# Small attention values of a fused attention and mixture-of-experts kernel held in free columns of a PSUM bank

## The chip, the cores and the metric

The kernel runs on one core of one Trainium2 chip. The metric is the device time of one execution in microseconds (us); less is better. The core has a matrix engine (TensorE, PE in the profile, PEld for its weight loads), a vector engine (VectorE, DVE), an activation engine (ScalarE, ACT), a general engine (GpSimd, POOL) and a queue engine (SyncE, SP) that issues most of the DMAs. TensorE writes to PSUM, a small memory of eight banks of 512 fp32 columns on 128 partitions; everything else lives in SBUF.

## The reference

Three stages follow each other. Only the first is touched by the change.

```python
# 1 attention: B=4, H=8, 512 local and 32 global positions, head size 64, window 32
s_g = scale * q_g @ concat(k_g, k_l).T            # global queries see all keys
out_g = softmax(s_g) @ concat(v_g, v_l)
s_l = concat(scale * q_l @ k_g.T, where(|i-j| <= 32, scale * q_l @ k_l.T, -1e9))
out_l = softmax(s_l) @ concat(v_g, v_l)           # softmax divides by sum + 1e-9
# 2 experts: 2176 tokens of 512, 8 experts, one expert a token
logits = x @ w_gate; e = argmax(logits)
y = probs[e] * (relu(x @ w1[e]) @ w2[e])
# 3 dense layer 512 -> 2048 -> 512
h = y @ w_in; g = h if h >= 1 else 0 if h <= -1 else (h + 1)**2 / 4
return g @ w_out
```

## The kernel before

Everything is written out by hand: the order of the instructions on TensorE, VectorE, ScalarE and SyncE is the order of the Python code, and a recording layer adds the waits between engines. Each engine works through its own list in order, so a waiting instruction holds up all that stand behind it on that engine.

The attention runs over 32 heads (`h`, one batch entry and head each) and 8 groups of four heads' global queries (`g`). The list `units` puts them into one sequence, and a loop over it issues for each unit pieces of several units, so that the engines work on different heads at one time. The pieces that matter here:

- `s_pair` (L253, L256): TensorE makes the scores of two heads in a PSUM tile `sp`, the mask added last.
- `s_max` (L262, L263): VectorE takes four row maxima of a head's 512 columns into `mx`, and turns them into the biases `mn` of the exponentials.
- `s_exp` (L280): ScalarE makes the exponentials `p` of a head in four instructions, and the sums `ss`.
- `t_head` (L335, L336): TensorE turns `p`, and VectorE copies the result out of PSUM to `pto`.
- `pv` (L380 to L385): TensorE multiplies with the values into `xo`; VectorE adds 1e-9 to the sums, takes the reciprocals `ri`, and multiplies `xo` by them.
- `s_glob`, `g_max`, `g_exp`, `g_norm`, `t_glob`, `pv_glob` (L292, L303 to L305, L316, L322 to L324, L346, L347, L356 to L359): the same for the global queries of a group; `pv_glob` is 24 small products on TensorE into `gxb`, then one multiplication on VectorE.
- `spread_v` (L225 to L227): GpSimd makes shifted copies of the values `v`, three in a row for a pair of heads.
- `route` (L457 to L466): nine steps on VectorE that make the chosen expert and its weight from a batch entry's logits, one of them with an exponential `ex` on ScalarE (L461). They wait in a list `fill`, of which up to eight are issued at the end of a unit.
- `ranks` (L491 to L494): TensorE counts tokens by expert into `gxb`.

`gxb` is one PSUM bank that stays allotted through the attention. Before, four things lie in it: columns 0 to 63 the last global scores (`s_glob`), 128 to 191 the output of `pv_glob`, from 256 on the counts of `ranks`, and 448 to 455 the logits of the global tokens. The recording layer orders accesses to such a tile by the bank, not by columns: an instruction that touches `gxb` waits for the last one on another engine that touched it and stands ahead of it in the code, where one of the two writes.

Of the sequence in one unit, two places matter: `s_max` of a head stands ahead of `pv_glob`, and `t_head` with `s_pair` ahead of both:

```python
        if kind == "h" and a < 31 and a != 3:
            s_max(a)
...
        for q in pend_g:
...
            pv_glob(q)
        for c in pend_v:
            pv(c)
```

After the attention (some 130 us), the expert stage and the dense layer follow, in which TensorE is busy nearly all the time.

Of the kernel before, what the change touches and what calls it, by code (L numbers as in the profile page):

```python
# [8 lines left out]
F32 = mybir.dt.float32  # L9
# [15 lines left out]
B, H, SL, SG, D = 4, 8, 512, 32, 64  # L25
# [8 lines left out]
E, F = 8, 1024  # L34
# [89 lines left out]
def emit(tc, d, out):  # L124
    nc = tc.nc
# [9 lines left out]
    def C(name):  # L135
        lo, hi = COFF[name]
        return csp[:, lo:hi] if hi <= CP else cst[:, lo - CP:hi - CP]
# [35 lines left out]
    ap = at.enter_context(tc.tile_pool(name="ap", bufs=1))  # L173
    ps = at.enter_context(tc.tile_pool(name="ps", bufs=1, space=PSUM))

    ks, vt, pt, ss = {}, {}, {}, {}
# [16 lines left out]
    def dma(o, i):  # L193
        t = nc.sync.dma_start(o, i)
        n = 1
        for z in o.shape:
            n *= z
        moved.append((t, n / 2**17))
        room = ROOM
        for u, n in reversed(moved):  # L200
            room -= n
            if room < 0 and u is not t:
                tc.add_manual_dep(t.ins, u.ins.name, mybir.DependencyInfo(mybir.DependencyClass.Sync, mybir.DependencyReason.DATA), reason="paced")
                break
        return t
# [23 lines left out]
    def v_at(j):  # L229
        g, t = divmod(j, 3)  # L230
        return (NW, 0, 2 * NW)[t] + g
# [10 lines left out]
    gxb = ps.tile([128, 512], F32, name="gxb")  # L242
# [14 lines left out]

    def s_max(n):
        sp = sps[n]
        mx = ap.tile([128, 4], F32, tag="mx4", name="mx4", bufs=2)  # L260
        mn = ap.tile([128, 4], F32, tag="mn", name="mn", bufs=3)
        nc.vector.tensor_reduce(mx, sp, axis=AX.X, op=ALU.max)  # L262
        nc.vector.tensor_single_scalar(mn, mx, -scale, op=ALU.mult)  # L263
        smn[n] = mn
# [101 lines left out]
    L4 = ap.tile([128, 5, 8], F32, name="L4")  # L366
    Lg = L4[:, 4, :]

    def pv(c):
        b, g = divmod(c, 4)  # L370
        p, v = pt.pop(c), vt[c]
        if g == 0:
            xr[b] = ap.tile([128, 4, DM], F32, tag="xr", name="xr", bufs=2)
            xT[b] = ap.tile([128, 4, SL], F32, tag="xT", name="xT", bufs=2)
        xo = ps.tile([128, 4, 2, D], F32, tag="s" if c == 15 else "x", name="xo", bufs=3 if c == 15 else 1)
        for i in range(4):
            for z in range(2):
                for a in range(4):
                    j = 4 * i + a
                    nc.tensor.matmul(xo[a * WIN:(a + 1) * WIN, i, z, :], lhsT=p[:, z, j * WIN:(j + 1) * WIN],  # L380
                                     rhs=v[:, v_at(j), 64 * z:64 * z + 64], start=True, stop=True)
        r = ap.tile([128, 4, 2], F32, tag="ri", name="ri", bufs=3)
        nc.vector.tensor_scalar_add(r, ss[b][:, :, 2 * g:2 * g + 2], 1e-9)
        nc.vector.reciprocal(r, r)
        nc.vector.tensor_tensor(xr[b][:, :, g * 128:(g + 1) * 128].rearrange("p i (z d) -> p i z d", z=2), xo,  # L385
                                r.unsqueeze(3).to_broadcast([128, 4, 2, D]), ALU.mult)

# [59 lines left out]
    def route(b):  # L447
        nt = 4 if b < B - 1 else 5
        t0 = 4 * b
        L = ap.tile([128, 5, 8], F32, tag="L", name="L", bufs=2)[:, 0:nt] if b < B - 1 else L4  # L450
        mx = ap.tile([128, 5, 1], F32, tag="mx", name="mx", bufs=2)[:, 0:nt]
        sc = ap.tile([128, 5, 8], F32, tag="sc", name="sc", bufs=2)[:, 0:nt]
        m2 = ap.tile([128, 5, 1], F32, tag="m2", name="m2", bufs=2)[:, 0:nt]
        ex = ap.tile([128, 5, 8], F32, tag="ex", name="ex", bufs=2)[:, 0:nt]
        se = ap.tile([128, 5, 1], F32, tag="se", name="se", bufs=2)[:, 0:nt]
        V = nc.vector
        ops = [lambda: V.tensor_reduce(L[:, 0:4], lgt[b][:, :, :, 0:E].rearrange("p i c e -> p i e c"), axis=AX.X, op=ALU.add)]  # L457
        rank_b = C("rank").unsqueeze(1).to_broadcast([128, nt, 8])
        ops += [lambda: V.tensor_reduce(mx, L, axis=AX.X, op=ALU.max),
                lambda: V.tensor_tensor(L, L, mx.to_broadcast([128, nt, 8]), ALU.subtract),  # L460
                lambda: (nc.scalar.activation(ex, L, AF.Exp), V.scalar_tensor_tensor(sc, L, 0.0, rank_b, ALU.is_ge, ALU.mult)),  # L461
                lambda: V.tensor_reduce(m2, sc, axis=AX.X, op=ALU.max),
                lambda: V.tensor_tensor(oh[:, t0:t0 + nt, :], sc, m2.to_broadcast([128, nt, 8]), ALU.is_equal),
                lambda: V.tensor_reduce(se, ex, axis=AX.X, op=ALU.add),
                lambda: V.tensor_scalar_add(se, se, 1e-9),
                lambda: (V.reciprocal(gid[:, t0:t0 + nt, 0:1], se),  # L466
                         dma(xs[b * SL:b * SL + nt * 128, DM:XW].rearrange("(i p) f -> p i f", p=128),
                                           gid[:, t0:t0 + nt]))]
        return ops
# [169 lines left out]
    for s in range(len(units)):  # L639
# [23 lines left out]
        if (kind, a) == ("g", 0):  # L663
            s_max(3)
        if kind == "h" and a < 31 and a != 3:
            s_max(a)
        if kind == "h" and a == 30:
            s_max(31)
        elif kind == "g":
            g_max(a)  # L670
# [6 lines left out]
        for c in pend_v:  # L677
            pv(c)
            if nv < 16:
                load_v(nv)  # L680
                nv += 1
            if 0 < c < 14:
                spread_v(c + 2)
            b, g = divmod(c, 4)
            if g % 2:
                tasks.append(lambda b=b, g=g: x_store(b, g // 2))
            tasks.append(lambda b=b, g=g: x_turn(b, g))
            if b < B - 1 and g == 3:
                then = [lambda b=b: tasks.append(lambda: early(b))]
                tasks += [lambda b=b: logits(b), lambda b=b: logits_t(b),  # L690
                          lambda b=b, then=then: fill.extend(route(b) + then)]
# [15 lines left out]
    weigh(xz, 128, nc.gpsimd)  # L707
    t_head(30)
    pv(14)
    t_head(31)  # L710
    for t in tasks:
        t()
    dma(xs[B * SL:N, 0:DM], xrg)
    glob_turn()
    pv(15)
    x_turn(B - 1, 2)
    x_store(B - 1, 1)
# [6 lines left out]
    part3()  # L724
    logits3_t()
    last = route(B - 1)
    for op in last[:6]:
        op()
# [23 lines left out]
    sc = rp.tile([128, NB], F32, name="sc")  # L752
# [716 lines left out]
```

## Time and profile before

| | |
|---|---|
| median of 3 runs | 740.49 us (738.86 to 744.5) |
| the profiled execution's own time | 741.64 us |
| its span, first to last instruction | 739.8 us |
| PE busy | 711.3 us (96%) |
| DVE busy | 486.1 us (66%) |
| ACT busy | 332.1 us (45%) |
| POOL busy | 150.2 us (20%) |
| mean granted TensorE clock | 0.992 of full |

Busy times are of the profiled execution. A busy TensorE is not one at its peak, since matmuls overlap. The chain that ended last names for each moment what was waited for; work of other engines beside it costs nothing. "issue" in that chain is time in which an engine waited for nothing that the profile shows. The time of an execution is its span and some 2 us around it.

### The profile page before, as it was taken

To read this page: it belongs to the slowest core of one execution; us is meant where nothing else is said; L and a number is where in the kernel's file an instruction comes from. 1 tells how busy PE (TensorE), PEld (TensorE's weight loads), DVE (VectorE), ACT (ScalarE), POOL (GpSimd) and SP (SyncE) were. 2 spreads that over 40 slices of the span, in tenths; PEclk is the share of its full clock that TensorE was granted. 3 is DMA by queue.
4 is the path that set the end of the run, shared out by engine and by line. 5 is a ranking of instruction groups with operands and counts; after the bars stand their busy time and mean duration, and the time that the engine had idled before them with its cause. 6 is when DMAs were issued, how large, how long until landed. Compare 5 with 4: busy or idle time off the path is not lost.

```text
span 739.8 us, 16419 instructions
## 1 busy us (share of the span) xinstructions
PE 711.3 (96%) x6609; PEld 637.6 (86%) x6609; DVE 486.1 (66%) x887; ACT 332.1 (45%) x762; POOL 150.2 (20%) x185
## 2 busy tenths in 40 slices
PE   6889888999999999999999999999999999999995
PEld 4666666999999999899998898999989898998984
DVE  4778885674516478875777678758775876645443
ACT  4757664453525457664564543233323332322220
POOL 3445543677641340000000000000000000011112
PEclk9999999999999999999999999999999999999998
DMA  8786666485658578763531321101110100001111
GB/s 280 237 258 202 203 194 186 134 291 196 190 166 301 199 252 305 244 208 104 122 99 58 105 68 57 58 1 58 57 58 1 58 0 1 1 30 57 43 43 71
DMA packets 52254, 96.07 MB, mean 130 GB/s; under 512 B 9817, under 2 KB 27769, under 8 KB 50128
## 3 DMA queue, kind: packets, MB, share of 16 engines
q1 hardware_dynamic: 48704, 84.75, 36.1%
q0 software_dynamic: 3472, 10.25, 4.2%
q8 instruction: 53, 0.87, 0.5%
q14 instruction: 25, 0.20, 0.1%
HBM read 80.28 MB, written 14.75 MB: 128 GB/s over the span
## 4 chain that ended last, share of the span: by engine, by line
PE 79%; issue 8%; DVE 7%; ACT 2%; DMA 2%; POOL 1%; SPq 0%; POOLq 0%; ACTq 0%; DVEq 0%
PE fh L988 7%; PE fh L986 7%; PE fh L987 7%; PE o L988 6%; PE o L987 6%; PE o L986 6%; PE hp L988 4%; PE hp L986 4%; PE hp L987 4%; PE yp L986 4%; PE yp L987 4%; PE yp L988 4%; PE ps_o L335 2%; PE sp L253 2%; DMA ks<-in_k 2%
## 5 line engine op out<-in xcount | busy, mean ns | idle before, releaser
L1318 DVE SCALAR_TENSOR_TENSOR r<-r 128x384 f32<-128x384 f32 (+1 forms) x96 | 51.4, 535 | 113.4 <-ACT r L1317 113.4
L986 PE MATMUL o<-wh,gh 128*128 128x512 f32 x272 | 106.9, 393 | 0.8 <-ACT acc L1367 0.8
L988 PE MATMUL o<-wh,gl 128*128 128x512 f32 x272 | 107.6, 396 | 0.0
L987 PE MATMUL o<-wl,gh 128*128 128x512 f32 x272 | 107.3, 394 | 0.0
L1371 POOL DMA_INDIRECT out_dram<-acc,rid x17 | 16.5, 969 | 446.4 <-DVE acc L1369 444.8
L1320 ACT ACTIVATE gh<-g 128x384 fp32r<-128x384 f32 (+1 forms) x96 | 48.8, 508 | 129.2 <-DVE g L1319 129.2
L988 PE MATMUL fh<-yh,wl 128*128 128x384 f32 (+1 forms) x320 | 104.3, 326 | 0.0
L986 PE MATMUL fh<-yh,wh 128*128 128x384 f32 (+1 forms) x320 | 104.2, 326 | 0.0
L987 PE MATMUL fh<-yl,wh 128*128 128x384 f32 (+1 forms) x320 | 104.2, 326 | 0.0
L1317 ACT ACTIVATE r<-fh,half 128x384 f32<-128x384 f32 (+1 forms) x96 | 54.0, 562 | 105.6 <-PE fh L988 105.0
L986 PEld LDWEIGHTS fh<-yh,wh 128*128 128x128 f32 x320 | 60.2, 188 | 3.5
L987 PEld LDWEIGHTS fh<-yl,wh 128*128 128x128 f32 x320 | 60.2, 188 | 3.4
L988 PEld LDWEIGHTS o<-wh,gl 128*128 128x128 f32 x272 | 51.1, 188 | 12.4 <-DVE gl L1326 0.4
L988 PEld LDWEIGHTS fh<-yh,wl 128*128 128x128 f32 x320 | 60.2, 188 | 0.0
L986 PEld LDWEIGHTS o<-wh,gh 128*128 128x128 f32 x272 | 51.1, 188 | 9.1 <-ACT acc L1367 1.2
L987 PEld LDWEIGHTS o<-wl,gh 128*128 128x128 f32 x272 | 51.1, 188 | 8.1
L280 ACT ACTIVATE p<-sp,mn 128x128 f32<-128x128 f32 x128 | 45.2, 373 | 20.0 <-DVE mn L263 10.1
L1319 DVE TENSOR_TENSOR g<-r,fh 128x384 f32<-128x384 f32 (+1 forms) x96 | 51.0, 532 | 3.3
L986 PE MATMUL yp<-hTh,w2h 128*128 128x256 f32 (+5 forms) x176 | 51.7, 294 | 0.0
L988 PE MATMUL yp<-hTh,w2l 128*128 128x256 f32 (+5 forms) x176 | 51.2, 291 | 0.0
L987 PE MATMUL yp<-hTl,w2h 128*128 128x256 f32 (+5 forms) x176 | 51.1, 290 | 0.0
L1326 DVE TENSOR_TENSOR gl<-g,gh 128x384 fp32r<-128x384 f32 (+1 forms) x96 | 50.7, 529 | 0.0
(238 smaller groups left out, 1617.3 us busy)
## 6 DMA issues: line engine op xcount, KB each, us to landing
w1r<-in_w SPq DMA_DIRECT2D x32, 512.0 KB
w2r<-in_w SPq DMA_DIRECT2D x32, 512.0 KB
wraw<-in_wf SPq DMA_DIRECT2D x16, 1024.0 KB
ks<-in_k SPq DMA_DIRECT2D x16, 400.0 KB
v<-in_v SPq DMA_DIRECT2D x16, 384.0 KB
yr<-ys SPq DMA_DIRECT2D x68, 64.0 KB
qp<-in_q SPq DMA_DIRECT2D x16, 256.0 KB
xs<-xr SPq DMA_DIRECT2D x8, 512.0 KB
```

The costliest lines, as they stand in the source:

```text
L253: nc.tensor.matmul(sps[2 * c + z][a * WIN:(a + 1) * WIN, i, :], lhsT=q[r, j * WIN:(j + 1) * WIN], rhs=k_at(k, r, j), start=(i == 0), stop= ...
L280: nc.scalar.activation(p[:, i, :].rearrange("p (a b w) -> p a b w", a=2, b=2), v, AF.Exp, bias=mn[:, i:i + 1], scale=scale, accum_out=ss[b ...
L335: nc.tensor.transpose(o[:, i, :], p[:, i, :], ident)
L986: nc.tensor.matmul(o, lhsT=ah, rhs=bh, start=first, stop=False)
L987: nc.tensor.matmul(o, lhsT=ah, rhs=bl, start=False, stop=False)
L988: nc.tensor.matmul(o, lhsT=al, rhs=bh, start=False, stop=last)
L1317: nc.scalar.activation(r[:, 0:w], o[:, 0:w], AF.Relu, bias=half, scale=0.5)
L1318: nc.vector.scalar_tensor_tensor(r[:, 0:w], r[:, 0:w], 1.0, r[:, 0:w], ALU.min, ALU.mult)
L1319: nc.vector.tensor_tensor(g[:, 0:w], r[:, 0:w], o[:, 0:w], ALU.max)
L1320: nc.scalar.activation(gh[:, 0:w], g[:, 0:w], AF.Copy)
L1326: nc.vector.tensor_tensor(gl[:, 0:w], g[:, 0:w], gh[:, 0:w].bitcast(F32), ALU.subtract)
L1371: w = nc.gpsimd.indirect_dma_start(out=out, out_offset=bass.IndirectOffsetOnAxis(ap=rid[:, tt:tt + 1].bitcast(U32), axis=0), in_=a, in_off ...
```

## The change

Four SBUF tiles of VectorE's small operations become columns of `gxb`: the row maxima of `s_max` (64 to 71, two sets in turn), the sums with 1e-9 added in `pv` (72 to 79; the reciprocals `ri` stay in SBUF), and in `route` the scores `sc` (80 to 119) and, of the first three batch entries, the logits `L` (192 to 223, one set where there were two). No instruction is added, taken away or reordered on TensorE, VectorE, ScalarE or SyncE. On GpSimd, whose order is not written by hand, the four small copies behind the third `pv_glob` (L362) now stand behind the second copy of a `spread_v` (L226), and before stood ahead of it. From L383 on, lines have a number that is higher by one than before.

```diff
     def s_max(n):
         sp = sps[n]
-        mx = ap.tile([128, 4], F32, tag="mx4", name="mx4", bufs=2)
+        mx = gxb[:, 64 + 4 * (n % 2):68 + 4 * (n % 2)]
         mn = ap.tile([128, 4], F32, tag="mn", name="mn", bufs=3)
...
         r = ap.tile([128, 4, 2], F32, tag="ri", name="ri", bufs=3)
-        nc.vector.tensor_scalar_add(r, ss[b][:, :, 2 * g:2 * g + 2], 1e-9)
-        nc.vector.reciprocal(r, r)
+        e = gxb[:, 72:80].rearrange("p (i z) -> p i z", i=4)
+        nc.vector.tensor_scalar_add(e, ss[b][:, :, 2 * g:2 * g + 2], 1e-9)
+        nc.vector.reciprocal(r, e)
...
-        L = ap.tile([128, 5, 8], F32, tag="L", name="L", bufs=2)[:, 0:nt] if b < B - 1 else L4
+        L = gxb[:, 192:224].rearrange("p (t e) -> p t e", e=E) if b < B - 1 else L4
         mx = ap.tile([128, 5, 1], F32, tag="mx", name="mx", bufs=2)[:, 0:nt]
-        sc = ap.tile([128, 5, 8], F32, tag="sc", name="sc", bufs=2)[:, 0:nt]
+        sc = gxb[:, 80:80 + nt * E].rearrange("p (t e) -> p t e", e=E)
```

What it moves is waits, since VectorE now writes a bank that TensorE writes too. Two places show it. The first is TensorE's list at the fourth `pv_glob`, behind the counts of `ranks` (58.4 us in the profile before); DVE, PE and so on with a number are the semaphores by which an engine tells how far it is, DMAHW those of the loads. Before:

```order
L494 LDWEIGHTS ones
L494 MATMUL gxb<-oh,ones 128x8
L356 MATMUL gxb<-v,pgt 32x64 [waits DMAHW2_49]
L356 MATMUL gxb<-v,pgt 32x64
L356 MATMUL gxb<-v,pgt 32x64 [waits DMAHW0_49]
L356 MATMUL gxb<-v,pgt 32x64 x13
```

And in the change:

```order
L495 LDWEIGHTS ones
L495 MATMUL gxb<-oh,ones 128x8
L356 MATMUL gxb<-v,pgt 32x64 [waits DMAHW2_49,DVE_49]
L356 MATMUL gxb<-v,pgt 32x64
L356 MATMUL gxb<-v,pgt 32x64 [waits DMAHW0_49]
L356 MATMUL gxb<-v,pgt 32x64 x13
```

The first product of `pv_glob` waits for VectorE now: for the `s_max` that stands ahead of it in the code, that is until L263 has read the maxima out of `gxb`. Of the eight `pv_glob`, numbers 1 to 5 and 7 (from 0) have this wait; numbers 0 and 6 wait on VectorE as before.

The second place is VectorE's list in the `route` of the first batch entry (51.4 us in the profile before). Before:

```order
L457 TENSOR_REDUCE L<-lg 128x32
L459 TENSOR_REDUCE mx<-L 128x4 [waits DVE_49]
L460 TENSOR_TENSOR L<-L,mx 128x32 [waits DVE_49]
L461 SCALAR_TENSOR_TENSOR sc<-L,cst 128x32 [waits DMAHW3_49,DVE_49]
L462 TENSOR_REDUCE m_1047<-sc 128x4 [waits DVE_49]
L463 TENSOR_TENSOR oh<-sc,m_1047 128x32 [waits DVE_49]
L464 TENSOR_REDUCE se<-ex 128x4 [waits Activation_49]
L465 TENSOR_SCALAR se<-se 128x4 [waits DVE_49]
```

And in the change:

```order
L458 TENSOR_REDUCE gxb<-lg 128x32
L460 TENSOR_REDUCE mx<-gxb 128x4 [waits DVE_49]
L461 TENSOR_TENSOR gxb<-gxb,mx 128x32 [waits DVE_49]
L462 SCALAR_TENSOR_TENSOR gxb<-gxb,cst 128x32 [waits DMAHW3_49,Activation_49]
L463 TENSOR_REDUCE m_1033<-gxb 128x4 [waits DVE_49]
L464 TENSOR_TENSOR oh<-gxb,m_1033 128x32 [waits DVE_49]
L465 TENSOR_REDUCE se<-ex 128x4
L466 TENSOR_SCALAR se<-se 128x4 [waits DVE_49]
```

The wait for ScalarE's exponential has moved three steps forward, from the sum `se` to the scores, since the exponential reads the bank that the scores are written to.

## Rows read from the trace of the kernel before

**Rows 1.** After the attention: us; PE, PEld, DVE, ACT, POOL busy; granted clock; DMA
```profile
130.00:739.80 609.80, 600.58 (x3587) 556.05 (x3585) 392.47 (x619) 254.37 (x414) 92.17 (x79) 1.00 0.34 110
```

**Rows 2.** Chain that ended last, in order of time: start, us, what (attention)
```profile
41.63 0.93 PE gxb L356 x46
...
47.29 1.93 issue
...
58.41 1.31 PE gxb L356 x48
...
73.76 0.59 PE ps_o L335 x4
...
87.28 0.81 PE gxb L356 x48
...
89.15 0.94 PE sp L292 x16
...
113.61 0.81 PE gxb L356 x48
114.63 1.41 issue
```

**Rows 3.** VectorE's instructions in order of time: start, us, line, output and input
```profile
34.92 0.63 DVE L263 TENSOR_SCALAR mn<-mx 128x4 f32<-128x4 f32 x1
...
42.30 0.24 DVE L263 TENSOR_SCALAR mn<-mx 128x4 f32<-128x4 f32 x1
...
51.95 0.81 DVE L460 TENSOR_TENSOR L<-L,mx 128x32 f32<-128x32 f32 x1
...
54.42 0.17 DVE L465 TENSOR_SCALAR se<-se 128x4 f32<-128x4 f32 x1
...
59.66 0.17 DVE L263 TENSOR_SCALAR mn<-mx 128x4 f32<-128x4 f32 x1
...
73.23 0.17 DVE L263 TENSOR_SCALAR mn<-mx 128x4 f32<-128x4 f32 x1
...
88.53 0.17 DVE L263 TENSOR_SCALAR mn<-mx 128x4 f32<-128x4 f32 x1
...
108.34 0.82 DVE L263 TENSOR_SCALAR mn<-mx 128x4 f32<-128x4 f32 x1
...
115.08 0.17 DVE L263 TENSOR_SCALAR mn<-mx 128x4 f32<-128x4 f32 x1
...
117.99 0.15 DVE L525 TENSOR_SCALAR zt<-n 128x1 f32<-128x1 f32 x1
...
118.65 0.15 DVE L537 TENSOR_SCALAR zidx<-ip 128x1 int32<-128x1 f32 x1
```

**Rows 4.** GpSimd's instructions in order of time, 50 to 56 us
```profile
51.89 0.82 POOL L225 COPY v<-v 96x768 f32<-96x768 f32 x1 [3.35 <-DMA v<-in_v]
...
53.53 0.72 POOL L227 COPY v<-v 64x640 f32<-64x640 f32 x1
```

**Rows 5.** One line's instructions each: least, median and most ns; first and last start
```profile
L263 DVE TENSOR_SCALAR mn<-mx x32: 169/170/821, 7.0 to 115.1; 128x4 f32<-128x4 f32 x32
...
L336 DVE COPY pto<-ps_o x32: 653/681/693, 10.7 to 121.7; 128x512 f32<-128x512 f32 x32
...
L461 ACT ACTIVATE ex<-L x4: 229/230/236, 52.8 to 128.8; 128x32 f32<-128x32 f32 x3, 128x40 f32<-128x40 f32 x1
```

**Rows 6.** All engines in order of time, 34 to 38 us
```profile
34.25 0.88 PE L356 MATMUL gxb<-v,pgt 128*32 128x64 f32 x48
...
35.67 0.37 ACT L280 ACTIVATE p<-sp,mn 128x128 f32<-128x128 f32 x1 [1.49 <-DVE mn L263]
...
36.18 1.37 PE L335 MATMUL ps_o<-ident,p 128*128 128x128 f32 x4
```

**Rows 7.** Busy time in two stretches of 4 us, columns as in rows 1
```profile
54.00:58.00 4.00, 1.91 (x57) 1.33 (x41) 3.72 (x12) 2.37 (x11) 1.07 (x3) 1.00 0.42 131
58.00:62.00 4.00, 4.00 (x75) 2.75 (x77) 3.45 (x11) 3.40 (x17) 2.68 (x7) 0.57 0.88 252
```

## The prediction

> **What bounds the kernel now.** I read the busy times by stage first, then the chain of waits through the attention, then the lists of VectorE and GpSimd side by side. After the attention TensorE is busy 600.58 of 609.80 us [rows 1]. That stage has no slack, and the change touches nothing in it, so it moves as a whole by what the attention's end moves. The 130 us before it are the only place where the change can act. There the chain jumps between TensorE and VectorE [rows 2]: products, then a row maximum, then exponentials, then products again. VectorE is on the path where it does a `route`, TensorE in nearly all the rest. So the question is not how much VectorE saves, but where it saves it, and which engine has to wait in exchange.
>
> **What the change can take away.** L263 works on four columns and has a median of 170 ns, yet one of its 32 took 821 ns [rows 5]. The step L460 took 0.81 us, and began right behind a copy of values on GpSimd (51.89 to 52.71, a batch of three that ends at 54.25) [rows 3, 4]; the other long ones lie under such copies too. These steps read and write SBUF alone. L336, which reads 512 columns of PSUM and writes SBUF, stays within 653 to 693 ns over 32 executions, although GpSimd is copying through many of them [rows 5]. From this I take it that a small step with an operand in PSUM is no longer held by GpSimd. What that is worth, place by place:
>
> - L263 at 108.34 took 0.82 us [rows 3] and its exponentials are waited for: 0.82 − 0.17 = 0.65 us gained on the path.
> - L263 at 34.92 took 0.63 us [rows 3]: 0.46 us gained, which the next part spends.
> - In `route` of the first two entries L460 and two steps behind it are stretched. Once they are short, L461 meets its new wait for `ex`, and L465, which stays in SBUF, meets GpSimd's third copy, which ends at 54.25; it began at 54.42 [rows 3, 4]. Only some 0.15 us is left of each, 0.3 us for both. In the third entry nothing was stretched, and the wait for `ex` (0.23 us [rows 5], plus 0.1 us until VectorE sees it) costs 0.33 us.
> - The other stretched L263 and L383 are beside the path. I cost them at nothing, covered by the loads of keys up to 16 us and by TensorE's own work later; uncovered, they would be a gain of at most 0.3 us each.
>
> Together: −0.65 − 0.3 + 0.33 = −0.6 us.
>
> **What it adds: waits.** Six of the eight `pv_glob` now wait until L263 of the `s_max` ahead of them has read the bank. Behind the waiting product stands everything of TensorE: `pv`, `t_head`, the next scores. From the end of an L263 to the engine that it releases takes some 0.1 us (34.92 + 0.63 = 35.55, ScalarE starts at 35.67 [rows 3, 6]). With L263 at its short 0.17 us, a `pv_glob` can start 0.27 us after L263's start:
>
> - Number 1: 34.92 + 0.27 = 35.19, it started at 34.25 [rows 3, 6]: 0.94 us late. But the `t_head` behind it had slack: it stood at 36.18 for 1.37 us because it was fed one exponential at a time [rows 6], where an unhindered one takes 0.59 us [rows 2], and the exponentials now come 0.46 us earlier. I take +0.1 us.
> - Number 2: 42.30 + 0.27 = 42.57 against 41.63: +0.9 us [rows 2, 3]. [...] I take 0, and keep 0.9 for the range.
> - Number 3: 59.66 + 0.27 = 59.93 against 58.41: 1.5 us [rows 2, 3]. [...] I take +0.75 us, and 1.5 as the end.
> - Number 4: 73.23 + 0.27 + 0.93 (as long as number 2) = 74.43, where the `t_head` behind it started at 73.76: +0.7 us [rows 2, 3].
> - Number 5: 88.53 + 0.27 + 0.81 + 0.59 for `t_head` = 90.20, where the step behind started at 89.15: +1.05 us [rows 2, 3]. The `t_head` gave some slack here too, and this is counted.
> - Number 7: 115.08 + 0.27 = 115.35 against 113.61: 1.74 us, of which an "issue" gap of 1.41 us right behind it [rows 2, 3] may swallow all but 0.35. I take +0.35, and 1.74 as the end.
>
> Sum: 0.1 + 0 + 0.75 + 0.7 + 1.05 + 0.35 = +2.95 us, with an upper end of 0.1 + 0.9 + 1.5 + 0.7 + 1.05 + 1.74 = 6.0 us.
>
> Smaller waits: an L383 right behind an L263 now waits for its end, since both touch the bank, at three places on the path. That costs less than L263's 0.17 us each, I take 0.1, so +0.3 us. The first `s_max` after a `g_exp` waits for ScalarE to have read `gxb`, and the products of `s_glob` and `ranks` wait for VectorE. By the times of before, what they wait for is done in time, or TensorE stands there anyway, since VectorE's `route` is late. So I cost them at nothing; if that cover goes, it is once what number 3 costs. GpSimd's exchange of two copies is covered by the loads that the values wait for.
>
> **What a PSUM operand costs VectorE.** Some 52 of the changed instructions lie on the path (14 pairs of L262 and L263, three pairs of L383 and L384, 18 of the three `route`). For a read the nearest rows are L525 and L537, one column each, from SBUF and from PSUM: 0.15 us both [rows 3]. For a write by VectorE the trace has no row. I take zero for both. For the bounds: 0.02 us less each, as between L263's 0.17 and L537's 0.15 [rows 3], is −1.0 us; 0.05 us more each, an estimate of a third of such a step, is +2.6 us.
>
> [...]
>
> **Sum.** −0.6 + 2.95 + 0.3 = +2.65 us. Made against the profiled execution that is 741.64 + 2.65 = 744.3 us, which lay 1.15 us above the median of its runs; against the median it is 740.49 + 2.65 = 743.1, and **743 us** is my forecast. A measurement of this kernel can tell about 1%, 7.4 us, from no change, so the forecast is a change too small for it, on the slow side.
>
> **Rivals.**
>
> 1. *Faster by a little: the waits are hidden.* TensorE gets its time back in the slack of `t_head`, in the two "issue" gaps and at low clock, and only the freed steps remain: −0.6, another −1.0 if a step with PSUM is 0.02 us shorter, and −0.9 for three more L263 that turn out to be on the path. 740.5 − 2.5 = 738 us. For it: both gaps stand right behind a delayed place. Against: behind numbers 4 and 5 the chain goes on with TensorE's own steps, at 73.76 and 89.15 [rows 2], and those have no slack to give.
> 2. *Slower beyond 1%: a write to PSUM is dear.* The place is L262, L383 and `route`, 52 steps on the path. At 0.1 us more each it is 743.1 + 5.2 = 748.3 us; from 0.09 us each on, the whole is over 1%. For it: no row shows such a write. Against: reads of PSUM show no price.
> 3. *The low clock moves.* It fell behind four microseconds in which TensorE was busy for 1.91 [rows 7]. If the new wait at 88 us, which also stands behind a `route`, brings one more such stretch, it costs what this one did, (1 − 0.57) × 4 = 1.7 us [rows 7]: 744.8 us.
> 4. *It does not do what it says:* GpSimd holds the steps as before. Then −0.65, −0.3 and the 0.46 of number 1 are not gained: 744.5 us.
>
> **How the numbers follow.** Chances: the forecast 0.52, rival 1 0.20, rival 2 0.08, rival 3 0.12, rival 4 0.08. The range goes from 739 (a little above rival 1's time) to 749 (the sum with all waits at their upper end, 743.1 + 3.05, and the dear end of the PSUM steps, +2.6, just covers rival 2). Faster by over 1% would need 7.4 us, more than all freed steps on the path hold: 0.04. Slower by over 1% is rival 2 and a share of rival 3 with all waits at their upper end: 0.12. Within 1%: 0.84.
>
> **What would show it.** In the profile after: L263 and L461 without an execution over 0.3 us; idle time of TensorE ahead of L356, released by L263, some 1 to 1.5 us at numbers 2, 3, 4, 5 and 7, and none at 0 and 6; the "issue" gaps shorter by what stands ahead of them; the stage after the attention the same length as before and begun some 2 to 3 us later. The prediction is wrong if the gaps keep their length behind a delay (then 1 to 2 us more), if L262 with its output in PSUM differs from 0.69 us, or if L336 between two `s_max` comes late and moves all maxima.

## The result and the profile after

The change takes 748.48 us (median of 7, 747.96 to 749.87) against 741.5 us (median of 7, 736.27 to 744.5) of the kernel before: ratio 1.0081, interval 1.0053 to 1.0108, that is +6.0 us, from 3.9 to 8.0. The profiled execution took 748.3 us with a span of 746.1. So it is slower, by 0.8% (0.5 to 1.1), and by more than the forecast +2.65 us.

After the attention nothing moved. In the windows of the changed kernel's profile (columns as in [rows 1]) the last stage is as long and as busy as before, and begins some 6 us later:

```profile
136.00:746.10 610.10, 600.97 (x3594) 556.55 (x3593) 392.88 (x620) 254.24 (x414) 92.21 (x79) 1.00 0.34 110
```

The small steps of VectorE do what the change says. Lines of the changed kernel, each with its count, the shortest, median and longest duration in ns, first and last start:

```profile
L263 DVE TENSOR_SCALAR mn<-gxb x32: 161/161/164, 8.2 to 121.4; 128x4 f32<-128x4 f32 x32
L262 DVE TENSOR_REDUCE gxb<-sp x32: 679/691/700, 7.4 to 120.6; 128x4 f32<-128x512 f32 x32
L461 DVE TENSOR_TENSOR gxb<-gxb,mx x3: 199/200/200, 57.2 to 112.9; 128x32 f32<-128x32 f32 x3
L462 DVE SCALAR_TENSOR_TENSOR gxb<-gxb,cst x3: 199/199/200, 57.9 to 113.4; 128x32 f32<-128x32 f32 x3
L466 DVE TENSOR_SCALAR se<-se x4: 163/170/694, 58.7 to 136.9; 128x4 f32<-128x4 f32 x3, 128x5 f32<-128x5 f32 x1
```

L263 took up to 821 ns before [rows 5] and takes 164 at most now; the step of `route` that took 0.81 us [rows 3] takes 0.20. L466, which stayed in SBUF, is still held once, for 694 ns.

What stands against it is on TensorE. The list of waits up to 136 us (engine and line, what it waited for: us in all, times, longest):

```profile
PEld gxb L356 <- DVE mn L263: 5.7, 4, 1.6
PE gxb L356 <- DVE mn L263: 4.7, 5, 1.5
```

These are the products of numbers 1 to 7 in the list of TensorE's instructions, where the 24 products of one `pv_glob` stand as 48 matmuls (start, us, line, output and input, count; in brackets the idle time before and what ended it):

```profile
41.53 0.88 PE L356 MATMUL gxb<-v,pgt 128*32 128x64 f32 x48 [0.99 <-DVE mn L263]
...
49.07 0.88 PE L356 MATMUL gxb<-v,pgt 128*32 128x64 f32 x48 [0.36 <-DVE mn L263]
...
64.28 0.88 PE L356 MATMUL gxb<-v,pgt 128*32 128x64 f32 x48 [1.48 <-DVE mn L263]
...
78.37 0.88 PE L356 MATMUL gxb<-v,pgt 128*32 128x64 f32 x48 [0.36 <-DVE mn L263]
...
94.09 0.88 PE L356 MATMUL gxb<-v,pgt 128*32 128x64 f32 x48 [1.48 <-DVE mn L263]
...
107.69 0.86 PE L356 MATMUL gxb<-v,pgt 128*32 128x64 f32 x48
...
121.70 0.88 PE L356 MATMUL gxb<-v,pgt 128*32 128x64 f32 x48 [1.80 <-ACT p L280]
```

TensorE stands ahead of six of them, 6.5 us in all, and not ahead of number 6. At numbers 2 and 4 it is 0.36 us, where the prediction said 1 to 1.5. At number 7 the profile names ScalarE's exponentials, but by VectorE's list the last L263 ends at 121.59, and the products start 0.1 us behind it:

```profile
121.43 0.16 DVE L263 TENSOR_SCALAR mn<-gxb 128x4 f32<-128x4 f32 x1
```

TensorE also stands 0.85 us for an L263 at the last `ranks` in this stretch (L492, 115.20 us). This cost nothing, as predicted: behind it TensorE waits for VectorE's L336 in both profiles, and it is 6.42 us late ahead of the place and 5.99 behind it.

To see what stays of the six waits, I compare the start of the same matmuls in both profiles: how late TensorE is just ahead of the place, at the place, and at the next group behind it that has no slack. For number 5 these are the lines of before (L395 has the number L396 in the change):

```profile
86.08 0.66 PE L395 MATMUL ps_x<-ident,xr 128*128 128x128 f32 x4 [1.90 <-DVE pto L336]
...
87.21 0.88 PE L356 MATMUL gxb<-v,pgt 128*32 128x64 f32 x48
...
89.08 1.01 PE L292 MATMUL sp<-ks,qg 64*32 64x320 f32 x16
```

And beside the 94.09 above, those of the change:

```profile
91.41 0.66 PE L396 MATMUL ps_x<-ident,xr 128*128 128x128 f32 x4 [0.27 <-DVE pto L336]
...
95.48 1.01 PE L292 MATMUL sp<-ks,qg 64*32 64x320 f32 x16
```

| `pv_glob` | late ahead of it | its start is late by | late behind it | added | forecast |
|---|---|---|---|---|---|
| 1 | 6.22 (L256) | 7.3 | 6.33 (L253) | +0.11 | +0.1 |
| 2 | 6.81 (L395) | 7.65 | 7.38 (L292) | +0.57 | 0, by the gap behind it |
| 3 | 4.39 (L395) | 5.9 | 4.98 (L292) | +0.59 | +0.75 |
| 4 | 4.91 (L395) | 5.75 | 5.48 (L292) | +0.57 | +0.7 |
| 5 | 5.33 (L395) | 6.9 | 6.41 (L292) | +1.08 | +1.05 |
| 7 | 5.98 (L253) | 8.2 | 6.56 (L395) | +0.58 | +0.35 |

At numbers 1, 3, 4 and 5 the forecast holds within 0.2 us, and without number 2 the places add 2.9 us, where 2.95 were forecast. But the profile after is 6.2 us late before the first wait of the change comes at all, and gives only part of that back: behind number 2 the lateness falls from 7.38 to 5.21, since the "issue" gap of 1.93 us [rows 2] is not there any more. These are TensorE's instructions at that place in the changed kernel (start, us, line, output and input, count), 64 products without a gap:

```profile
53.72 1.16 PE L253 MATMUL sp<-ks,qp 64*32 64x128 f32 x64
54.81 0.50 PE L256 MATMUL sp<-mask 128*128 128x384 bf16 x2
```

About half of the early lateness is the clock. It fell to its lower level (0.50 of full at 110 to 112 us in the profile before) three times in the attention after (around 12, 36 and 118 us) and twice before (60 and 110 us), each time for some 3.4 us, which is 1.7 us of work. The windows of the changed kernel around 34 us show one, behind two microseconds without a single matmul (the last numbers are granted clock, DMA share, GB/s):

```profile
32.00:34.00 2.00, 0.00 (x0) 0.00 (x0) 1.52 (x5) 2.00 (x13) 0.61 (x1) 1.00 0.85 285
34.00:36.00 2.00, 1.93 (x11) 1.59 (x10) 0.69 (x1) 0.47 (x3) 0.41 (x1) 0.61 1.12 327
36.00:38.00 2.00, 2.00 (x26) 1.04 (x26) 0.11 (x1) 0.55 (x2) 1.84 (x3) 0.54 0.81 237
```

The stretches at 12 and 36 us lie ahead of the first of the new waits in front of `pv_glob`, at 41.53 us, so these waits did not bring them. Nor can the early lateness be put down to the change. These are the starts of the same L256, the one ahead of number 1, in two profiles of the kernel before (the second is before_again below), in mx_sbuf, an experiment below in which TensorE has none of these waits, and in the change:

```profile
33.82 0.50 PE L256 MATMUL sp<-mask 128*128 128x384 bf16 x2
...
35.35 0.50 PE L256 MATMUL sp<-mask 128*128 128x384 bf16 x2
...
37.47 0.50 PE L256 MATMUL sp<-mask 128*128 128x384 bf16 x2
...
40.04 0.50 PE L256 MATMUL sp<-mask 128*128 128x384 bf16 x2
```

In mm_first, another experiment, which has all four operands in the bank, it starts at 33.05. So one pair of profiles cannot say how much of the 6 us is the change and how much is chance. The experiments had to.

### The profile page after: what moved, and what is told of

It is laid out like the page before. It is cut to its first block, busy times and chain, and to the rows that moved or that the text cites. A ratio compares the mean times of both kernels' runs of the same rounds, so it can differ in the third digit from the quotient of the medians.

```text
span 746.1 us, 16432 instructions
## 1 busy us (share of the span) xinstructions
PE 714.6 (96%) x6609; PEld 638.2 (86%) x6609; DVE 481.0 (64%) x887; ACT 331.6 (44%) x762; POOL 150.2 (20%) x185
## 4 chain that ended last, share of the span: by engine, by line
PE 79%; issue 8%; DVE 7%; ACT 3%; POOL 1%; DMA 1%; SPq 0%; POOLq 0%; ACTq 0%; DVEq 0%
PE fh L989 7%; PE fh L987 7%; PE fh L988 7%; PE o L989 6%; PE o L988 6%; PE o L987 6%; PE hp L989 4%; PE hp L987 4%; PE hp L988 4%; PE yp L987 4%; PE yp L989 4%; PE yp L988 4%; PE ps_o L335 2%; PE sp L253 2%; PE xo L380 1%
## 5 line engine op out<-in xcount | busy, mean ns | idle before, releaser
L1319 DVE SCALAR_TENSOR_TENSOR r<-r 128x384 f32<-128x384 f32 (+1 forms) x96 | 51.4, 535 | 113.4 <-ACT r L1318 113.4
```

Of the source, the lines that this page charges most:

```text
L1319: nc.vector.scalar_tensor_tensor(r[:, 0:w], r[:, 0:w], 1.0, r[:, 0:w], ALU.min, ALU.mult)
```

## The experiments

All times are medians; the ratio is to the kernel before on the same chip; the clock is the mean over the executions of the granted TensorE clock over the whole span. Over its 87 executions on the three chips of the experiments the kernel before has 742.4 us on average and a clock of 0.9917.

| kernel | us | ratio (interval) | clock |
|---|---|---|---|
| the change | 748.48 | 1.0081 (1.0053 to 1.0108) | 0.9886 |
| before_again | 742.43 | 0.9989 (0.9956 to 1.0023) | 0.9925 |
| waits_only | 747.78 | 1.0077 (1.0047 to 1.0107) | 0.9872 |
| mx_only | 747.88 | 1.0062 (1.0028 to 1.0096) | 0.9885 |
| mx_sbuf | 741.71 | 0.9998 (0.9960 to 1.0036) | 0.9922 |
| wait_127 | 742.53 | 1.0004 (0.9976 to 1.0032) | 0.9939 |
| wait_345 | 748.20 | 1.0050 (1.0013 to 1.0086) | 0.9883 |
| glob_first | 745.64 | 1.0034 (0.9998 to 1.0070) | 0.9904 |
| mm_first | 743.76 | 1.0019 (0.9991 to 1.0047) | 0.9923 |
| waits_again | 752.07 | 1.0114 (1.0076 to 1.0153) | 0.9855 |
| fill_all | 749.84 | 1.0097 (1.0066 to 1.0128) | 0.9925 |
| fill_345 | 747.13 | 1.0055 (1.0027 to 1.0082) | 0.9925 |
| fill_rank | 743.20 | 1.0024 (0.9994 to 1.0054) | 0.9928 |

### Is it the wait, the operands, or the freed steps?

The kernel before, unchanged, for the spread:

> The kernel before, unchanged, for a second trace of it. Theory 1 (TensorE's waits for VectorE at the bank make the 6 us): the time is that of the kernel before, 741 us, and the start of the attention, up to the first products of scores behind the first global group (L253 at 16.6 us in the first trace, 18.9 us in the change), lies between the two or at either, by chance of the first loads. Theory 2 (the change moves the start: 2.3 of its 6.3 us are there by 17 us, before the first new wait that holds TensorE): this second trace starts like the first, 16.6 us, and the change alone starts late.

It agrees with itself within 0.5%. Its L253 of theory 1 starts at 17.45 us, between the 16.6 and the 18.9, so the start varies without the change; and although its L256 above comes 1.5 us later than in the first profile, its attention ends 3.0 us earlier (first L573 at 124.88 us, where it was 127.84). Next, the wait without the change: all small steps in SBUF as before, and a dependency added.

```diff
+    last = [None]
-        nc.vector.tensor_single_scalar(mn, mx, -scale, op=ALU.mult)
+        last[0] = nc.vector.tensor_single_scalar(mn, mx, -scale, op=ALU.mult)
...
-                nc.tensor.matmul(go[h * SG:(h + 1) * SG], lhsT=pgt[q][:, m, h * SG:(h + 1) * SG],
+                w = nc.tensor.matmul(go[h * SG:(h + 1) * SG], lhsT=pgt[q][:, m, h * SG:(h + 1) * SG],
...
+                if m == 0 and h == 0 and q not in (0, 6):
+                    tc.add_manual_dep(w.ins, last[0].ins.name, ...)
```

> The kernel before with everything in SBUF, and one dependency added: the first product of each pv_glob but numbers 0 and 6 waits for the L263 of the maxima ahead of it. Theory 1 (this wait is the price): the sum of the six waits, 3 to 6 us, so 744 to 747 us, and TensorE stands ahead of each of the six. Theory 2 (the start, or the operands in PSUM): within 1.5 us of the kernel before, since the six waits are swallowed by gaps that are there anyway.

747.78 us: the wait alone costs 5.7 us (3.5 to 7.9), what the change costs. Then mx_only, the kernel before with the maxima alone in the bank, and mx_sbuf, the change with the maxima alone put back. The edit of mx_only is one line, and that of mx_sbuf is the same line turned round:

```diff
     def s_max(n):
         sp = sps[n]
-        mx = ap.tile([128, 4], F32, tag="mx4", name="mx4", bufs=2)
+        mx = gxb[:, 64 + 4 * (n % 2):68 + 4 * (n % 2)]
```

> Of the change only the row maxima lie in the bank; sums, scores and logits stay in SBUF. Theory 1: nearly the whole loss, 746 to 749 us, since the six waits come from the maxima. Theory 2 (route and sums carry it, by the wait for the exponential and the waits of VectorE on itself): about half, 743 to 745 us or less.

> The change with the row maxima back in SBUF; sums, scores and logits stay in the bank. Theory 1: the six waits are gone, and the loss with them: 739 to 743 us, on either side of the kernel before, as GpSimd holds route no longer. Theory 2: the loss stays, 744 us or more.

747.88 against 741.71 us, with intervals that meet only between 1.0028 and 1.0036: the loss goes with the maxima. With the maxima in SBUF, `route` and the sums in the bank bring neither a price nor a gain that this interval (0.9960 to 1.0036) can tell. The lines of mx_sbuf tell the two kinds of step apart within one execution: its L263, in SBUF again, is held up to 733 ns, and its L461 in the bank never.

```profile
L263 DVE TENSOR_SCALAR mn<-mx x32: 170/171/733, 7.3 to 115.5; 128x4 f32<-128x4 f32 x32
L461 DVE TENSOR_TENSOR gxb<-gxb,mx x3: 199/199/199, 53.5 to 107.0; 128x32 f32<-128x32 f32 x3
```

### Which places, and does the gap swallow?

The wait-only kernel again, with the wait at three places each (`q in (1, 2, 7)` and `q in (3, 4, 5)`).

> Kernel before with all small steps in SBUF, and the wait of the first product for L263 of the row maxima ahead of it put in at pv_glob 1, 2 and 7 alone. These are the three places whose price the prediction took as swallowed: +0.45 us together, 3.6 us if nothing is swallowed. Theory A (the issue gaps at 47 and 114 us end at a fixed time and swallow what stands ahead of them): 741.5 to 742.5 us, ratio 1.000 to 1.001, both gaps shorter by about 0.9 and 1.4 us. Theory B (the gaps are as long as before behind a delay; the three places are the missing 3 us of the sum): 744.5 to 745.5 us, ratio 1.004 to 1.005, gaps of 1.9 and 1.4 us. Theory C (the waits bring more stretches at the low clock, each 1.7 us): three stretches or more in the record instead of two, wherever the waits are.

> Kernel before with all small steps in SBUF, and the same wait at pv_glob 3, 4 and 5 alone. The prediction's price of these is 0.75 + 0.7 + 1.05 = 2.5 us, 3.25 with number 3 at its full 1.5. Theory A (these three carry the loss, and 1, 2, 7 are swallowed): the whole loss of the wait-only kernel, 6 us: 747 us, ratio 1.006 to 1.008. Theory B (priced rightly here, the rest comes from 1, 2 and 7): 744 us, ratio 1.003 to 1.004. Theory C (each group adds low-clock stretches of 1.7 us): a third stretch in the record, and 745 to 746 us.

Numbers 1, 2 and 7 cost +0.3 us (from −1.8 to +2.4), numbers 3 to 5 cost +3.7 by the ratio (1.0 to 6.4). Theory B, that the three swallowed places are the missing part, is not borne out. The gaps are shorter in the profile of wait_127, as theory A has it: 1.03 us behind number 2, where it was 1.93 [rows 2], and behind number 7 0.39, where it was 1.41. (The wait at number 7, too, is put down to ScalarE.) But they are shorter also where no product waits, none and 0.89 us in before_again, 0.26 and 0.55 in mx_sbuf. So it is shown that these places cost little, and not that the gaps took the delay. The lines of wait_127 behind number 7:

```profile
115.52 0.88 PE L358 MATMUL gxb<-v,pgt 128*32 128x64 f32 x48 [1.80 <-ACT p L282]
...
117.01 0.94 PE L384 MATMUL xo<-v,pto 128*32 128x64 f32 x50 [0.39 <-issue]
```

In wait_345 the two long waits are visible in the same view, 1.96 us at number 3 and 1.76 at number 5. (L265, its name for L263, works in SBUF here and lay under a copy of GpSimd both times, 0.65 and 0.45 us long; so the waits of the wait-only kernels can be longer than the change's.) The lines:

```profile
60.01 0.88 PE L358 MATMUL gxb<-v,pgt 128*32 128x64 f32 x48 [1.96 <-DVE mn L265]
...
90.82 0.88 PE L358 MATMUL gxb<-v,pgt 128*32 128x64 f32 x48 [1.76 <-DVE mn L265]
```

And right behind each of them its windows show the lower clock, which the profile before has at one of these places only (60 us [rows 7]):

```profile
62.00:64.00 2.00, 2.00 (x48) 1.33 (x44) 1.86 (x6) 0.00 (x0) 1.51 (x4) 0.50 0.17 61
...
90.00:92.00 2.00, 1.18 (x51) 1.09 (x52) 0.89 (x3) 1.68 (x11) 1.43 (x2) 1.00 1.08 295
92.00:94.00 2.00, 2.00 (x23) 0.89 (x25) 1.81 (x8) 0.36 (x3) 1.40 (x5) 0.51 0.79 285
```

That is theory C's mark: three stretches at the lower clock in the attention of wait_345, none in wait_127, and clocks of 0.9883 against 0.9939 over 12 executions each. So not every wait lowers the clock: those at numbers 1, 2 and 7 did not. The time of wait_345 fits the theories A, B and C alike within its interval.

### Is it TensorE that must not wait?

Two kernels turn the wait round: the products stand ahead of `s_max`, so TensorE goes on and VectorE waits for the bank. In glob_first the whole of `pv_glob` is moved up; in mm_first its 48 matmuls are, as a function of their own, and its copy L359 on VectorE stays behind `s_max`.

```diff
+        for q in pend_g:
+            if gq == ("g", q):
+                continue
+            pv_glob(q)
         if (kind, a) == ("g", 0):
             s_max(3)
...
-        for q in pend_g:
-            if gq == ("g", q):
-                continue
-            pv_glob(q)
```

> The change, with pv_glob written ahead of the s_max of the same unit. The order of TensorE stays, its wait for that unit's L263 is gone, and VectorE waits for the products instead: L359 and then L262 stand behind the last of 48 matmuls, so the maxima come 1.1 to 1.4 us later at the same places. Theory 1 (the price is TensorE standing at pv_glob): TensorE no longer idle there, the exponentials have 2 us of slack at most places and none at number 1, so 742 to 743 us, ratio 1.000 to 1.002. Rival (any wait on that bank is dear, on whichever engine): 746 to 748 us, with TensorE waiting at t_head for late exponentials.

> The change, with the 48 matmuls of pv_glob ahead of that unit's s_max, and its copy L359 on VectorE left behind s_max as it was. VectorE's L262 waits for the last matmul, 0.8 to 1.0 us later than in the kernel before, 0.3 us less than where the copy is moved too. Theory 1: 742 us, ratio 0.999 to 1.001, as good as the change with its maxima in SBUF (741.7). Rival (late maxima cost as much as a late product): 746 us or more.

TensorE's idle time ahead of `pv_glob` is gone in both. VectorE's waits in the list of mm_first:

```profile
DVE gxb L262 <- PE gxb L355: 7.3, 6, 2.5
```

In the change VectorE stood as long, at the copy L359 behind these products:

```profile
DVE xgo L359 <- PE gxb L356: 7.1, 7, 1.1
```

So 7.3 us of waiting on VectorE alone cost +1.4 us (1.0019, from −0.7 to +3.5), where 7.1 us on VectorE and 6.5 us on TensorE cost 6.0. Its interval ends at 1.0047 and that of the change begins at 1.0053. glob_first, with its copy ahead as well, makes the exponentials late for TensorE (3.9 us in four waits of L335, the second line below; the third line is the kernel before) and lies between: 1.0034, wide enough to be either.

```profile
DVE xgo L359 <- PE gxb L356: 8.1, 6, 2.1
PE ps_o L335 <- ACT p L280: 3.9, 4, 2.4
...
PE ps_o L335 <- ACT p L280: 1.9, 3, 1.0
```

### Does the clock fall because TensorE stands?

If so, giving TensorE useless work in the wait must bring the clock back. The 48 matmuls of `pv_glob` are issued twice; only the second set has the wait, and it overwrites the first. fill_all does it to the wait-only kernel, fill_345 to wait_345 (`q in (3, 4, 5)`).

```diff
+        if q not in (0, 6):
+            for m in range(NW):
+                for h in range(4):
+                    nc.tensor.matmul(go[h * SG:(h + 1) * SG], lhsT=pgt[q][:, m, h * SG:(h + 1) * SG],
+                                     rhs=vt[2 * q + h // 2][:, m, 64 * (h % 2):64 * (h % 2) + 64], start=(m == 0), stop=(m == NW - 1))
         for m in range(NW):
```

> The wait-only kernel once more (everything in SBUF, pv_glob 1 to 5 and 7 wait for L263), to stand beside the two filled kernels on one chip. So far: 747.8 us, ratio 1.0077, mean granted clock over its executions 0.987 where the kernel before has 0.992. Same again: 747 to 749 us, clock 0.986 to 0.989.

> The wait-only kernel, with the 48 matmuls of pv_glob issued twice at numbers 1 to 5 and 7: the first set has no wait and is overwritten by the second, whose first product waits for L263 as before. So TensorE computes 0.8 to 0.9 us of the 0.9 to 1.5 us in which it stood, and the products that count start at the same time as in the wait-only kernel, 0.1 us later at most where the wait was short. Theory C (half of the loss is that the clock falls more often because TensorE stands): clock back to 0.991 to 0.993, time 743.5 to 745.5 us, ratio 1.003 to 1.005; what stays is the lateness, 2.5 to 3 us. Rival D (the clock has nothing to do with the standing, or the price is all lateness): 747.5 to 749 us, clock 0.986 to 0.988.

> The kernel with the wait at pv_glob 3, 4 and 5 alone, filled in the same way at these three. Without the fill it had 748.2 us median (mean 747.5), ratio 1.005, clock 0.988. Theory C: clock 0.991 to 0.993, 744 to 745.5 us. Rival D: 747 to 749 us, clock 0.988.

waits_again missed its forecast: 752.07 us where 747 to 749 were expected, 8.5 us (5.6 to 11.4) above the kernel before, and a clock just below the range. The same kernel's two measurements, 1.0077 and 1.0114, agree only within their intervals.

The clock came back both times, to 0.9925: from 0.9855 (standard error 0.0010) in waits_again, which ran on the same chip, and from 0.9883 (0.0007) in wait_345, on another one. In the profile of fill_345 it is full behind numbers 3 and 5, where that of wait_345 above has the lower level:

```profile
62.00:64.00 2.00, 2.00 (x60) 1.35 (x51) 1.30 (x7) 1.06 (x7) 1.04 (x5) 1.00 0.89 305
...
92.00:94.00 2.00, 2.00 (x62) 1.44 (x66) 1.75 (x8) 0.61 (x4) 1.15 (x5) 1.00 0.79 239
```

The time did not follow as theory C had it: fill_all, at 749.84 us, is above the range of theory C and of rival D too, and only 2.2 us below waits_again, with intervals that overlap; fill_345 is within 1.1 us of wait_345 and lies where rival D said. The added matmuls may cost something of their own, which is not shown. The list of waits has time for which TensorE's weight loads stood for nothing visible ahead of `pv`. These are the lines of fill_all, of waits_again and of the kernel before:

```profile
PEld xo L389 <- issue: 7.3, 14, 1.8
...
PEld xo L384 <- issue: 3.0, 11, 1.3
...
PEld xo L380 <- issue: 4.3, 10, 1.6
```

In fill_345 that list shows no such growth (1.5 us in 9 times), so what its fill costs stays open.

The last kernel tried the same cure on the kernel before, at the place where it stands for VectorE behind `ranks` (107.8 us) and the clock falls at 109:

```diff
-        ranks(t0, t1, 1 if end else 0)
+        for _ in range(9 if end else 1):
+            ranks(t0, t1, 1 if end else 0)
```

> The kernel before with one addition, and no wait added: the six small matmuls of ranks in the third entry of route (L491 to L494, at 107.8 us) are issued nine times instead of once, each time from the start, so the result is the same. They fill 1.2 to 1.5 of the 1.85 us in which TensorE stands there for VectorE, behind which the clock fell at 109 us in the profile of before. Theory C (standing there brings the low clock): that stretch of 3.4 us at half clock is gone in most executions, clock 0.993 to 0.995, 740 to 741 us, ratio 0.998 to 0.999. Rival D: clock 0.992 and time as before, 742 us, or 0.3 us more if the added matmuls outlast the wait.

A miss: 743.2 us, clock 0.9928 where before has 0.9911 on that chip. TensorE stands for VectorE 0.57 us there, where it was 1.85 in the kernel before (the first line is fill_rank's, the second that of before):

```profile
107.66 1.33 PE L335 MATMUL ps_o<-ident,p 128*128 128x128 f32 x4 [0.57 <-DVE pto L336]
...
109.96 1.33 PE L335 MATMUL ps_o<-ident,p 128*128 128x128 f32 x4 [1.85 <-DVE pto L336]
```

But the windows of fill_rank's profile show the clock falling at the same place, behind two microseconds in which TensorE was busy for 1.43 us, some 1.1 of them with the small matmuls:

```profile
106.00:108.00 2.00, 1.43 (x46) 1.27 (x42) 1.97 (x5) 1.05 (x7) 1.89 (x3) 1.00 0.68 236
108.00:110.00 2.00, 1.96 (x46) 1.41 (x51) 1.83 (x10) 2.00 (x11) 0.67 (x2) 0.61 0.82 128
```

No version beats the kernel before beyond what can be told from no change; mx_sbuf and mm_first equal it within their intervals.

## Why the prediction was right, and where its size was off

The forecast was a change within 1% on the slow side, by TensorE's new waits in front of `pv_glob`. The measured ratio is on that side, its mechanism is the one named (waits_only and mx_sbuf show it), and the time lies inside the range. The size was 6.0 us where the sum said 2.65. That the range reached so far is luck: with all waits at their upper end the prediction came to 743.1 + 3.05 = 746.15 us, and only the 2.6 us for a dear PSUM operand, which the runs put at nothing, took it past 748.48.

- **What is taken away.** L263 and L461 have no execution over 0.2 us, so rival 4 is out. From the sum of the logits to the end of the L263 behind it, the three `route` took 3.97, 3.81 and 3.14 us before, and 3.01, 3.51 and 2.75 after: −0.96, −0.30 and −0.39 against −0.15, −0.15 and −0.32 said. The third copy on GpSimd caught L466 once out of three times, not each time. None of it is seen in the time of mx_sbuf, which has most of it: these gains and the spread of 0.4% are of one size. The 0.46 us at number 1 belonged to that one execution: L263 was not held there in before_again and mx_sbuf, and against them number 1 adds 0.57 and 0.59 us instead of 0.11.
- **The six waits.** Numbers 1, 3, 4 and 5 come out within 0.2 us of their terms in the pair of profiles. Number 1 owes that to the luck above. The 0.75 us for number 3, half of its 1.5, is a term that no run shows: the pair shows 0.59, with a granted clock of 0.57 of full there in the profile before [rows 7] and full in the change. Its matmuls L356 take 1.38 us before and 0.88 in the change, so at full clock in both it would have added about 1.1 us, an estimate (0.59 and that 0.5). Numbers 1, 2 and 7 alone cost +0.3 us in wait_127 against +0.45. The 0 taken for number 2 is a term that no run shows either: the pair shows 0.57 there. That an "issue" gap swallows a delay, on which the terms of numbers 2 and 7 rest, is not borne out (see the last section). Number 7 added 0.58 instead of 0.35. The +0.3 for L383 was not measured by itself.
- **A PSUM operand.** L262 takes 691 ns instead of 682, L263 161 instead of 170, the two steps of the sums 170 and 208 instead of 163 and 203: zero within 10 ns either way, which is the value taken. Rival 2 is out.
- **The term that was too small** is the one for the six waits, +2.95 us. waits_only, which has these waits and nothing else of the change, costs 5.7 us (3.5 to 7.9), and 8.5 when measured again; numbers 3 to 5 alone cost 3.7 (1.0 to 6.4), where 2.5 were said. In the pair of profiles the places themselves add 2.9 us, 3.5 with number 2, so what is missing is not to be seen there.
- **What the sum left out** is the lower clock. It stood as rival 3, with one more stretch, 1.7 us, and a chance of 0.12, as if it were an accident of one place. In the mean it is no accident: the five kernels with waits at numbers 3 to 5 and no fill have a clock of 0.9855 to 0.9886, the kernel before 0.9917. From the first of these waits to the end of the attention, and with a stretch of twice the length counted as two, the profile of the change has one stretch and the other four have three each; the kernel before, its repeat and mx_sbuf have two, one and one, fill_all none and fill_345 two. How much of the time that is, I can only estimate. Over 218 executions of all kernels, each taken against its own kernel's mean, a microsecond of clock lost ((1 − clock) times the span) goes with 0.80 us of time (standard error 0.07). By that slope the change's mean of +6.3 us (748.7 to 742.4) holds 1.9 us of clock and 4.4 of waiting; wait_345 2.0 and 3.0 (2.5 said); wait_127 −1.3 and 1.5 (0.45 said). By this estimate the waits were priced 0.5 to 2 us too low, of which the luck at number 1 is 0.5, and the clock was missing. But a slope does not tell a cause from what goes with it, and the fills, which gave the clock back and not the time, speak against it. What the missing 3 us are made of stays open.

That the clock falls because TensorE stands at these places is shown by the two fills (0.9925 with each, against 0.9855 on the same chip and 0.9883 on another without), though at another place, in fill_rank, a fill of smaller matmuls did not keep it up (0.61 of full from 108 to 110 us). That giving the clock back gives the time back is not: no fill did it, and the split above rests on the slope alone.

Of what was to show the prediction wrong, none came about: the gaps did not keep their length, L262 kept its 0.69 us, and L336 was not late at a price, since TensorE waited 3.0 us for it up to 136 us, and 6.9 before. But the last stage was to begin 2 to 3 us later, and began 6 us later.

## What to carry to other kernels

Scratch columns in a free part of a PSUM bank are not free if another engine writes that bank (they cost 6.0 us here): the ordering here is by the bank, so look for the instruction on the busiest engine that will now wait, and price its wait before the steps that are saved. When such a wait can't be avoided, write the code so that the engine with slack waits: 7.3 us of waiting on VectorE alone cost 1.4 us here, and with 6.5 us on TensorE beside it 6.0. And where TensorE is near its limit (96% busy here), a wait of 1 to 2 us on it can lower the clock behind it (to 0.50 and 0.51 of full behind the 1.96 and 1.76 us of wait_345), which may make it cost more than its length less the slack (the first is shown here, the second is not); count the clock of many executions, since one profile shows at most four such stretches in the attention, and some of them come by chance.

## What was not expected of the hardware

- Six waits of 0.4 to 1.8 us on TensorE lowered the mean granted clock of a 740 us kernel from 0.992 to 0.986 to 0.989, and those at numbers 1, 2 and 7 alone did not lower it (0.9939); 48 useless fp32 matmuls in each of the six brought it back to 0.9925, and nine sets of six small bf16 matmuls at another place did not keep it up there.
- GpSimd's copies stretch a 4-column step of VectorE from 0.17 to as much as 0.82 us (L263 at 108.34 us in the kernel before [rows 3], under a copy from 108.31 to 109.13) when both its operands are in SBUF, and never in these profiles when one is in PSUM (161 to 164 ns over the 32 of the change). Which step is hit changes from one execution to the next.
- An "issue" gap has no length of its own, and no fixed end: the one of 1.93 us in the profile before, from 47.29 to 49.22 us, was 0.26 us in mx_sbuf, and there was none in the change. It does not just take back lateness: fill_rank came there 0.6 us earlier than the kernel before and had 1.11 us, fill_345 came 2.2 us later and still had 1.55. In the lists of mx_sbuf, fill_rank and fill_345 (the gap stands in brackets):

```profile
49.53 0.95 PE L253 MATMUL sp<-ks,qp 64*32 64x128 f32 x49
50.73 0.45 PE L253 MATMUL sp<-ks,qp 64*32 64x128 f32 x15 [0.26 <-issue]
...
47.82 0.45 PE L253 MATMUL sp<-ks,qp 64*32 64x128 f32 x15 [1.11 <-issue]
...
51.05 0.45 PE L253 MATMUL sp<-ks,qp 64*32 64x128 f32 x15 [1.55 <-issue]
```
